# Transposing on the DMA crossbar in place of TensorE, in a fused linear-attention and MLP layer

## The chip, the cores and the metric

The kernel runs on one core of a Trainium2 chip. A core has five engines that run side by side, each with its own queue of instructions: TensorE (PE in the profile: matmuls and transposes; PEld is its loading of weights), VectorE (DVE), ScalarE (ACT), GpSimd (POOL) and SyncE (SP), which here only issues DMAs. The DMAs of a core share 16 DMA engines. Data lives in SBUF, 128 partitions wide; TensorE writes its results to PSUM, from where VectorE or ScalarE takes them. The metric is the device time of one execution, in microseconds (us), as a median of several runs.

## The reference

Input are 2048 tokens of 512 features, all in bf16. The tokens are normalised, and both branches read the normalised tokens:

```python
xn = layernorm(x)                                    # [2048, 512]
# branch A: linear attention, 32 heads of 16
q, k, v = split(xn @ wqkv)
phi(t)  = concat(softmax(t @ w_phi), softmax(-t @ w_phi))   # per head, 16 -> 32
kv, z   = phi(k).T @ v, sum over tokens of phi(k)    # per head, over all 2048 tokens
o       = (phi(q) @ kv) / (phi(q) @ z + 1e-6)        # [2048, 512]
# branch B: MLP with 1792 hidden units
h       = mish(xn @ w1 + b1)
out     = x + o @ wo + h @ w2
```

Since kv and z are sums over all tokens, no attention output can be made before the last token has been seen.

## The kernel before

The tokens are worked on in four groups of 512, each of four tiles of 128 tokens (TPG = 4). All weights stay in SBUF. There are two phases.

The first phase takes the groups in turn. `stage_ln(g)` makes the statistics of four tiles (L178, L179), the reciprocal deviations (L182, L186) and the normalised tile `xn`, tokens on partitions (L188). The matmuls need the features on partitions, so each `xn` of 128 x 512 is transposed by TensorE in four blocks of 128 x 128 (L197) into a PSUM bank `ptr`, and ScalarE copies two tiles at a time (L202) into `xnT`, one buffer per group, two buffers in turn. `xnT` is the weight operand of keys and values (`stage_kv_pair`, L252 and L267, two tiles of tokens at a time) and the moving operand, 512 tokens wide, of queries (`stage_q`, L328) and of the hidden layer (`stage_h`, L364, 56 matmuls a group). ScalarE makes the exponentials (L260, L261, L336, L337) and mish (L374); VectorE makes sums, reciprocals and products. `stage_kvacc` (L303) adds the group's share of kv and z. `stage_ln` of the next group is called between `stage_q` and `stage_kvacc` of the present one, so the next `xnT` is made while the hidden layer of the present group runs.

The second phase takes the groups again. `stage_o(g)` makes, per tile of 128 tokens, numerators and denominators (L389, eight matmuls, into one of the two double PSUM banks), a reciprocal (L398) and the product `o_t` (L400). The four `o_t` of a group are transposed by TensorE (L412, 16 transposes into two banks `ptro`) and copied by ScalarE (L417) into `oT`. `stage_out(g)` loads the group's tokens again for the residual (L422), and adds for each tile 14 matmuls with w2 (L427) and four with wo, whose weight operand is `oT` (L435), in one PSUM bank; VectorE adds the residual (L443), SyncE stores (L444).

The order in which each engine runs its instructions is fixed when the kernel is built, by the framework's scheduler, which starts from the order of the program and moves ready work forward into gaps; the waits between engines are put in by it too. ScalarE's functions are held in the order written (`chain`). The DMAs of the later token loads (L471), of the residuals (L422) and of the stores (L444) go through SyncE's queue, in order. The buffers of tokens (`xg`) are two, so a load waits until the tile that lay there has been read.

Of the kernel before, what the change touches and what calls it, by code (L numbers as in the profile page):

```python
# [8 lines left out]
BF16 = mybir.dt.bfloat16  # L9
# [8 lines left out]
def kernel(  # L18
# [12 lines left out]
    nc = tc.nc  # L31
    P = 128
    S, D, NH, DH, F = 2048, 512, 32, 16, 1792
    NG = 4
    TPG = 4
    NT = NG * TPG
    KT = D // P
# [22 lines left out]
    xnTpool = ctx.enter_context(tc.tile_pool(name="xnT", bufs=2))  # L60
# [15 lines left out]
    with nc.allow_non_contiguous_dma(reason="tiny w_phi load"):  # L76
# [19 lines left out]
    ident = consts.tile([P, P], BF16, name="ident")  # L96
# [8 lines left out]
        out=mask17[:],  # L105
        in_=mask17[:],
# [7 lines left out]
        out=mask17[:],  # L114
        in_=mask17[:],
# [46 lines left out]
    def bank_m(name, shape=None, dt=FP32):  # L162
        return ps_m.tile(shape or [P, 512], dt, name=name, tag="m")


    def stage_ln(g):
        xg = xgs[g]
        mv = spool.tile([P, TPG, nc.vector.BN_AGGR_DIM], FP32, name="mv")
        rstd = spool.tile([P, TPG], FP32, name="rstd")
        xnT = xnTpool.tile([P, KT, 512], BF16, name="xnT")  # L170
        step = 1 if g == 0 else TPG
        for t0 in range(0, TPG, 2):
            ptr = bank_m("ptr", [P, KT, 2 * P], BF16)
            for t in range(t0, t0 + 2):
                if t % step == 0:
                    for u in range(t, t + step):
                        st = spool.tile([P, nc.vector.BN_STATS_DIM], FP32, name="st")
                        nc.vector.bn_stats(st[:], xg[:, u, :])  # L178
                        nc.vector.bn_aggr(mv[:, u, :], st[:])  # L179
                    us = slice(t, t + step)  # L180
                    chain(
                        nc.scalar.activation(  # L182
                            rstd[:, us], mv[:, us, 1], ACT.Sqrt, bias=eps_t[:]
                        )
                    )
                    nc.vector.reciprocal(rstd[:, us], rstd[:, us])  # L186
                xn = xnpool.tile([P, D], BF16, name="xn")
                nc.vector.tensor_scalar(  # L188
                    out=xn[:],
                    in0=xg[:, t, :],  # L190
                    scalar1=mv[:, t, 0:1],
                    scalar2=rstd[:, t : t + 1],
                    op0=ALU.subtract,
                    op1=ALU.mult,
                )
                for kt in range(KT):
                    nc.tensor.transpose(  # L197
                        ptr[:, kt, (t - t0) * P : (t - t0 + 1) * P],
                        xn[:, kt * P : (kt + 1) * P],
                        ident[:],  # L200
                    )
            nc.scalar.copy(xnT[:, :, t0 * P : (t0 + 2) * P], ptr[:])  # L202
        return xnT


# [41 lines left out]
    def stage_kv_pair(xnT, pr):  # L247
        pk = big("pk")
        for tt in range(2):
            tok0 = (2 * pr + tt) * P  # L250
            for kt in range(KT):
                nc.tensor.matmul(  # L252
                    pk[:, tt, :],
                    lhsT=xnT[:, kt, tok0 : tok0 + P],
                    rhs=wkp[:, kt, :],
                    start=(kt == 0),
                    stop=(kt == KT - 1),
                )
        ek = ekpool.tile([P, 2, 2, 512], BF16, name="ek")
        chain(nc.scalar.activation(ek[:, 0], pk[:], ACT.Exp))  # L260
        chain(nc.scalar.activation(ek[:, 1], pk[:], ACT.Exp, scale=-1.0))  # L261
        v12s = []
        for tt in range(2):
            tok0 = (2 * pr + tt) * P
            pv = bank_v("pv")
            for kt in range(KT):
                nc.tensor.matmul(  # L267
                    pv[:],
                    lhsT=xnT[:, kt, tok0 : tok0 + P],
                    rhs=wv[:, kt, :],  # L270
                    start=(kt == 0),
                    stop=(kt == KT - 1),
                )
            ss = spool.tile([P, 2, NH], FP32, name="ss")
            nc.vector.reduce_sum(  # L275
                ss[:],
                ek[:, :, tt, :].rearrange("p s (h e) -> p s h e", e=DH),
                axis=AX.X,
            )
            rk = spool.tile([P, 2, NH], FP32, name="rk")  # L280
            nc.vector.reciprocal(rk[:], ss[:])
            v12 = vpool.tile([P, 2, NH, VW], BF16, name="v12")
            nc.vector.tensor_tensor(
                out=v12[:, :, :, 0:DH],
                in0=pv[:]
                .rearrange("p (o h e) -> p o h e", o=1, e=DH)
                .to_broadcast([P, 2, NH, DH]),
                in1=rk[:, :, :, None].to_broadcast([P, 2, NH, DH]),
                op=ALU.mult,
            )  # L290
            nc.gpsimd.tensor_copy(v12[:, :, :, DH], rk[:])
            v12s.append(v12)
        return ek, v12s
# [27 lines left out]
    def stage_q(g, xnT):  # L321
        gs = slice(g * 512, (g + 1) * 512)
        for jp in range(2):
            pq = big("pq")
            for jj in range(2):
                j = 2 * jp + jj
                for kt in range(KT):
                    nc.tensor.matmul(  # L328
                        pq[:, jj, :],
                        lhsT=wqp[:, kt, j * P : (j + 1) * P],  # L330
                        rhs=xnT[:, kt, :],
                        start=(kt == 0),
                        stop=(kt == KT - 1),
                    )
            eq = eqpool.tile([P, 2, 2, 512], BF16, name="eq")
            chain(nc.scalar.activation(eq[:, 0], pq[:], ACT.Exp))  # L336
            chain(nc.scalar.activation(eq[:, 1], pq[:], ACT.Exp, scale=-1.0))  # L337
            for jj in range(2):
                j = 2 * jp + jj
                for pl in range(2):  # L340
                    pS = bank_m("pS")
                    nc.tensor.matmul(  # L342
                        pS[:],
                        lhsT=B16b[:],
                        rhs=eq[:, 1 - pl, jj, :],
                        start=True,
                        stop=True,
                    )
                    nc.vector.tensor_tensor(  # L349
                        out=eqT[:, pl * 4 + j, gs],  # L350
                        in0=pS[:],
                        in1=eq[:, pl, jj, :],
                        op=ALU.mult,
                    )


    def stage_h(xnT, pool):
        act = pool.tile([P, FT, 512], BF16, name="act")
        for fp in range(FT // 2):
            ph = big("ph")  # L360
            for ff in range(2):
                f = 2 * fp + ff
                for kt in range(KT):
                    nc.tensor.matmul(  # L364
                        ph[:, ff, :],
                        lhsT=w1_sb[:, kt, f * P : (f + 1) * P],
                        rhs=xnT[:, kt, :],
                        start=(kt == 0),
                        stop=(kt == KT - 1),
                    )  # L370
            for ff in range(2):
                f = 2 * fp + ff
                chain(
                    nc.scalar.activation(  # L374
                        act[:, f, :], ph[:, ff, :], ACT.Mish, bias=b1f[:, f : f + 1]
                    )
                )
        return act


    def stage_o(g):
        oT = oTpool.tile([P, 4, 512], BF16, name="oT")
        o_ts = []
        for t in range(TPG):
            tok0 = g * 512 + t * P
            pnd = big("pnd")
# [16 lines left out]
                in1=rd[:, :, :, None].to_broadcast([P, 2, 16, DH]),  # L403
                op=ALU.mult,
            )
            o_ts.append(o_t)
        for jh in range(2):
            ptr = bank_m("ptro", [P, 2, 512], BF16)
            for t in range(TPG):
                for jj in range(2):  # L410
                    j = 2 * jh + jj
                    nc.tensor.transpose(  # L412
                        ptr[:, jj, t * P : (t + 1) * P],
                        o_ts[t][:, j * P : (j + 1) * P],
                        ident[:],
                    )
            nc.scalar.copy(oT[:, 2 * jh : 2 * jh + 2, :], ptr[:])  # L417
        return oT

    def stage_out(g, act, oT):  # L420
        xg2 = xpool.tile([P, TPG, D], BF16, name="xg")
        nc.sync.dma_start(xg2[:], x_g[g])  # L422
        for t in range(TPG):
# [10 lines left out]
            for j in range(4):  # L434
                nc.tensor.matmul(  # L435
                    po[:],
                    lhsT=oT[:, j, ts],
                    rhs=wo_sb[:, j, :],
                    start=False,
                    stop=(j == 3),  # L440
                )
# [81 lines left out]
```

## Time and profile before

| | us |
|---|---|
| median of 3 timed runs | 212.46 (212.35 to 212.74) |
| the profiled execution | 212.4 |
| its span, from the first to the last instruction | 210.7 |
| TensorE busy | 193.6 (92%) |
| VectorE busy | 117.8 (56%) |
| ScalarE busy | 104.5 (50%) |
| granted TensorE clock, mean | 0.997 of full speed |

A share of busy time is an average over the whole span. The chain that ended last tells which work set the end: it is followed back from the last instruction, at each step to what released it. A wait is idle time of an engine together with what ended it. The ends of matmuls are modelled and overlap, so the distance from one start to the next is the time that a matmul takes of TensorE.

### The profile page before, as it was taken

The page shows a single profiled execution, that of the slowest core. Times are in us where ns is not written, and L with a number is a line of the kernel's source. Part 1 is how long each engine was busy: PE and PEld are TensorE (multiplying, and loading weights), DVE is VectorE, ACT ScalarE, POOL GpSimd, SP SyncE. Part 2 cuts the span into 40 slices and gives each one's busy share as a digit, 9 for nine tenths or more (in the row PEclk, how much of TensorE's full clock was granted, in tenths as well). Part 3 has the DMA queues.
Part 4 walks back from the last instruction along what each step waited for, and adds up shares of the span by engine and source line. Part 5 has one row for each costly group of instructions (what it writes and reads, how often), then busy time and mean ns, then how long its engine had stood idle before and what let it go on. Part 6 is the DMA issues. An engine that isn't in the chain of part 4 may idle for free.

```text
span 210.7 us, 2908 instructions
## 1 busy us (share of the span) xinstructions
PE 193.6 (92%) x1185; PEld 98.0 (47%) x1185; DVE 117.8 (56%) x205; ACT 104.5 (50%) x133; POOL 8.6 (4%) x25
## 2 busy tenths in 40 slices
PE   0398899999989999989999999999999999999993
PEld 0364443564434644435643445644554464455441
DVE  1807799983998505997219985531352172136211
ACT  2565998558895768976589734430030003002100
POOL 2000010000110000110001100000000000000000
PEclk9999999999999999999999999999999999999998
DMA  5999500030000300000200000001030130100010
GB/s 170 342 370 348 170 0 0 2 103 0 2 0 0 102 0 0 0 3 1 98 0 3 0 2 0 3 0 50 28 124 25 50 124 4 50 25 28 25 50 25
DMA packets 12088, 12.25 MB, mean 58 GB/s; under 512 B 1068, under 2 KB 12076, under 8 KB 12076
## 3 DMA queue, kind: packets, MB, share of 16 engines
q1 hardware_dynamic: 10492, 11.02, 15.9%
q10 hardware_dynamic: 1584, 1.07, 1.8%
q8 instruction: 9, 0.15, 0.3%
q14 instruction: 3, 0.02, 0.0%
HBM read 9.98 MB, written 2.10 MB: 57 GB/s over the span
## 4 chain that ended last, share of the span: by engine, by line
PE 71%; ACT 10%; DVE 9%; DMA 7%; issue 1%; SPq 0%; ACTq 0%
PE po L427 23%; PE ph L364 18%; PE po L435 7%; DVE ss L275 5%; DMA xg<-in_A_x_dram 5%; PE pkv L303 4%; PE pnd L389 4%; PE pk L252 3%; PE pv L267 3%; PE pS L342 3%; DMA wk_raw<-in_A_wqkv_dram 2%; ACT ek L261 2%; PE ptro L412 2%; ACT eq L337 2%; PE pq L328 2%; PE ptr L197 1%
## 5 line engine op out<-in xcount | busy, mean ns | idle before, releaser
L364 PE MATMUL ph<-xnT,w_sb 128*128 128x512 bf16 x224 | 55.5, 379 | 1.4 <-ACT act L374 1.4
L427 PE MATMUL po<-w_sb,act 128*128 128x512 bf16 x224 | 54.4, 379 | 0.0
L374 ACT ACTIVATE act<-ph,b1f 128x512 bf16<-128x512 f32 x56 | 35.2, 686 | 22.9 <-PE ph L364 22.9
L443 DVE TENSOR_TENSOR y<-po,xg 128x512 bf16<-128x512 f32 x16 | 11.1, 692 | 46.8 <-PE po L435 46.8
L364 PEld LDWEIGHTS <-w_sb 128*128 128x128 bf16 x224 | 21.6, 98 | 27.2 <-issue 3.4
L417 ACT COPY oT<-ptro 128x1024 bf16<-128x1024 bf16 x8 | 7.7, 1015 | 53.5 <-PE ptro L412 53.5
L427 PEld LDWEIGHTS <-act 128*128 128x128 bf16 x224 | 21.3, 98 | 22.2
L275 DVE TENSOR_REDUCE ss<-ek 128x64 f32<-128x1024 bf16 x16 | 18.7, 1203 | 18.5 <-ACT ek L261 18.5
L349 DVE TENSOR_TENSOR eqT<-pS,eq 128x512 bf16<-128x512 f32 x32 | 20.6, 685 | 1.8 <-PE pS L342 1.6
L267 PE MATMUL pv<-wv,xnT 128*128 128x512 bf16 x64 | 17.3, 396 | 0.0
L435 PE MATMUL po<-wo_sb,oT 128*128 128x512 bf16 x64 | 17.2, 380 | 0.0
L328 PE MATMUL pq<-xnT,wqp 128*128 128x512 bf16 x64 | 15.1, 379 | 1.6 <-ACT ek L261 1.5
L178 DVE BATCH_NORM_STATS2 st<-xg 128x6 f32<-128x512 bf16 x16 | 10.4, 673 | 9.9 <-DMA xg<-in_A_x_dram 9.9
L252 PE MATMUL pk<-wkp,xnT 128*128 128x512 bf16 x64 | 15.8, 379 | 0.0
L197 PE MATMUL ptr<-ident,xn 128*128 128x128 bf16 x64 | 5.9, 243 | 8.7 <-DVE xn L188 8.7
L342 PE MATMUL pS<-eq,B16b 128*128 128x512 bf16 x32 | 11.6, 378 | 0.4 <-DVE eqT L349 0.4
L400 DVE TENSOR_TENSOR o_t<-pnd,rd 128x512 bf16<-128x512 f32 x16 | 11.1, 691 | 0.6
L328 PEld LDWEIGHTS <-wqp 128*128 128x128 bf16 x64 | 6.2, 97 | 9.7 <-issue 2.8
L267 PEld LDWEIGHTS <-xnT 128*128 128x128 bf16 x64 | 6.4, 102 | 7.2 <-issue 0.7
L435 PEld LDWEIGHTS <-oT 128*128 128x128 bf16 x64 | 5.6, 98 | 8.9 <-ACT oT L417 3.2
L389 PEld LDWEIGHTS <-eqT 128*128 128x128 bf16 x128 | 7.9, 98 | 3.8 <-DVE o_t L400 2.4
L389 PE MATMUL pnd<-kvm,eqT 128*128 128x136 bf16 x128 | 9.6, 223 | 0.0
(102 smaller groups left out, 199.2 us busy)
## 6 DMA issues: line engine op xcount, KB each, us to landing
xg<-in_A_x_dram SPq DMA_DIRECT2D x7, 512.0 KB, 3.8
out_dram<-y SPq DMA_DIRECT2D x16, 128.0 KB, 1.7
w_sb<-in_B_w_dram SPq DMA_DIRECT2D x2, 896.0 KB, 9.1
w_sb<-in_B_w_dram SPq DMA_DIRECT2D x1, 1792.0 KB, 14.7
wk_raw<-in_A_wqkv_dram ACTq DMA_DIRECT2D x1, 512.0 KB, 4.8
xg<-in_A_x_dram SPq DMA_DIRECT2D x2, 256.0 KB, 4.4
wv<-in_A_wqkv_dram SPq DMA_DIRECT2D x1, 512.0 KB, 7.6
wq_raw<-in_A_wqkv_dram ACTq DMA_DIRECT2D x1, 512.0 KB, 8.5
```

The lines of the kernel that those rows point to most:

```text
L252: nc.tensor.matmul(pk[:, tt, :], lhsT=xnT[:, kt, tok0 : tok0 + P], rhs=wkp[:, kt, :], start=(kt == 0), stop=(kt == KT - 1),)
L267: nc.tensor.matmul(pv[:], lhsT=xnT[:, kt, tok0 : tok0 + P], rhs=wv[:, kt, :], start=(kt == 0), stop=(kt == KT - 1),)
L275: nc.vector.reduce_sum(ss[:], ek[:, :, tt, :].rearrange("p s (h e) -> p s h e", e=DH), axis=AX.X,)
L328: nc.tensor.matmul(pq[:, jj, :], lhsT=wqp[:, kt, j * P : (j + 1) * P], rhs=xnT[:, kt, :], start=(kt == 0), stop=(kt == KT - 1),)
L342: nc.tensor.matmul(pS[:], lhsT=B16b[:], rhs=eq[:, 1 - pl, jj, :], start=True, stop=True,)
L349: nc.vector.tensor_tensor(out=eqT[:, pl * 4 + j, gs], in0=pS[:], in1=eq[:, pl, jj, :], op=ALU.mult,)
L364: nc.tensor.matmul(ph[:, ff, :], lhsT=w1_sb[:, kt, f * P : (f + 1) * P], rhs=xnT[:, kt, :], start=(kt == 0), stop=(kt == KT - 1),)
L374: nc.scalar.activation(act[:, f, :], ph[:, ff, :], ACT.Mish, bias=b1f[:, f : f + 1])
L389: nc.tensor.matmul(pnd[:, j // 2, (j % 2) * 136 : (j % 2) * 136 + 136], lhsT=eqT[:, pl * 4 + j, tok0 : tok0 + P], rhs=kvm[:, pl * 4 + j, : ...
L400: nc.vector.tensor_tensor(out=o_t[:].rearrange("p (a h e) -> p a h e", a=2, e=DH), in0=nd[:, :, :, 0:DH], in1=rd[:, :, :, None].to_broadca ...
L427: nc.tensor.matmul(po[:], lhsT=act[:, f, ts], rhs=w2_sb[:, f, :], start=(f == 0), stop=False,)
L435: nc.tensor.matmul(po[:], lhsT=oT[:, j, ts], rhs=wo_sb[:, j, :], start=False, stop=(j == 3),)
```

## The change

For groups 1 to 3 the four normalised tiles of a group, and for all groups the four `o_t`, are no longer transposed by TensorE and copied by ScalarE. Each tile of 128 x 512 goes through one DMA on SyncE's queue (`dma_start_transpose`) from SBUF to SBUF, transposed on the way. The first group's normalised tiles stay on TensorE. Since one DMA writes a whole tile, `xnT` and `oT` are laid out tile by tile: [128, tile, block of features, 128 tokens] in place of [128, block of features, 512 tokens]. The moving operand of L328 and L364 therefore becomes four runs of 128 columns.

```diff
--- before.py
+++ after.py
@@ -167,10 +167,10 @@
         xg = xgs[g]
         mv = spool.tile([P, TPG, nc.vector.BN_AGGR_DIM], FP32, name="mv")
         rstd = spool.tile([P, TPG], FP32, name="rstd")
-        xnT = xnTpool.tile([P, KT, 512], BF16, name="xnT")
+        xnT = xnTpool.tile([P, TPG, KT, P], BF16, name="xnT")
         step = 1 if g == 0 else TPG
         for t0 in range(0, TPG, 2):
-            ptr = bank_m("ptr", [P, KT, 2 * P], BF16)
+            ptr = bank_m("ptr", [P, 2, KT, P], BF16) if g == 0 else None
             for t in range(t0, t0 + 2):
                 if t % step == 0:
                     for u in range(t, t + step):
@@ -193,13 +193,15 @@
                     op0=ALU.subtract,
                     op1=ALU.mult,
                 )
+                if g > 0:
+                    nc.sync.dma_start_transpose(out=xnT[:, t], in_=xn[:])
+                    continue
                 for kt in range(KT):
                     nc.tensor.transpose(
-                        ptr[:, kt, (t - t0) * P : (t - t0 + 1) * P],
-                        xn[:, kt * P : (kt + 1) * P],
-                        ident[:],
-                    )
-            nc.scalar.copy(xnT[:, :, t0 * P : (t0 + 2) * P], ptr[:])
+                        ptr[:, t - t0, kt, :], xn[:, kt * P : (kt + 1) * P], ident[:]
+                    )
+            if g == 0:
+                nc.scalar.copy(xnT[:, t0 : t0 + 2], ptr[:])
         return xnT
 
 
@@ -247,11 +249,10 @@
     def stage_kv_pair(xnT, pr):
         pk = big("pk")
         for tt in range(2):
-            tok0 = (2 * pr + tt) * P
             for kt in range(KT):
                 nc.tensor.matmul(
                     pk[:, tt, :],
-                    lhsT=xnT[:, kt, tok0 : tok0 + P],
+                    lhsT=xnT[:, 2 * pr + tt, kt, :],
                     rhs=wkp[:, kt, :],
                     start=(kt == 0),
                     stop=(kt == KT - 1),
@@ -261,12 +262,11 @@
         chain(nc.scalar.activation(ek[:, 1], pk[:], ACT.Exp, scale=-1.0))
         v12s = []
         for tt in range(2):
-            tok0 = (2 * pr + tt) * P
             pv = bank_v("pv")
             for kt in range(KT):
                 nc.tensor.matmul(
                     pv[:],
-                    lhsT=xnT[:, kt, tok0 : tok0 + P],
+                    lhsT=xnT[:, 2 * pr + tt, kt, :],
                     rhs=wv[:, kt, :],
                     start=(kt == 0),
                     stop=(kt == KT - 1),
@@ -328,7 +328,7 @@
                     nc.tensor.matmul(
                         pq[:, jj, :],
                         lhsT=wqp[:, kt, j * P : (j + 1) * P],
-                        rhs=xnT[:, kt, :],
+                        rhs=xnT[:, :, kt, :],
                         start=(kt == 0),
                         stop=(kt == KT - 1),
                     )
@@ -364,7 +364,7 @@
                     nc.tensor.matmul(
                         ph[:, ff, :],
                         lhsT=w1_sb[:, kt, f * P : (f + 1) * P],
-                        rhs=xnT[:, kt, :],
+                        rhs=xnT[:, :, kt, :],
                         start=(kt == 0),
                         stop=(kt == KT - 1),
                     )
@@ -379,8 +379,7 @@
 
 
     def stage_o(g):
-        oT = oTpool.tile([P, 4, 512], BF16, name="oT")
-        o_ts = []
+        oT = oTpool.tile([P, TPG, 4, P], BF16, name="oT")
         for t in range(TPG):
             tok0 = g * 512 + t * P
             pnd = big("pnd")
@@ -403,18 +402,7 @@
                 in1=rd[:, :, :, None].to_broadcast([P, 2, 16, DH]),
                 op=ALU.mult,
             )
-            o_ts.append(o_t)
-        for jh in range(2):
-            ptr = bank_m("ptro", [P, 2, 512], BF16)
-            for t in range(TPG):
-                for jj in range(2):
-                    j = 2 * jh + jj
-                    nc.tensor.transpose(
-                        ptr[:, jj, t * P : (t + 1) * P],
-                        o_ts[t][:, j * P : (j + 1) * P],
-                        ident[:],
-                    )
-            nc.scalar.copy(oT[:, 2 * jh : 2 * jh + 2, :], ptr[:])
+            nc.sync.dma_start_transpose(out=oT[:, t], in_=o_t[:])
         return oT
 
     def stage_out(g, act, oT):
@@ -434,7 +422,7 @@
             for j in range(4):
                 nc.tensor.matmul(
                     po[:],
-                    lhsT=oT[:, j, ts],
+                    lhsT=oT[:, t, j, :],
                     rhs=wo_sb[:, j, :],
                     start=False,
                     stop=(j == 3),
```

## Rows read from the trace of the kernel before

**Rows 1.** The page's busy us, share of the span, instructions, by engine

```profile
PE 193.6 (92%) x1185; PEld 98.0 (47%) x1185; DVE 117.8 (56%) x205; ACT 104.5 (50%) x133; POOL 8.6 (4%) x25
```

**Rows 2.** The page's chain that ended last, shares of the span by engine

```profile
PE 71%; ACT 10%; DVE 9%; DMA 7%; issue 1%; SPq 0%; ACTq 0%
```

**Rows 3.** Stretches; columns as their header line says

```profile
core 0: us, PE busy (x) PEld busy (x) DVE busy (x) ACT busy (x) POOL busy (x), PEclk, DMA share, GB/s
47.30:76.40 29.10, 27.84 (x162) 13.63 (x161) 20.08 (x33) 22.38 (x28) 1.79 (x4) 1.00 0.06 19
151.10:169.80 18.70, 18.70 (x124) 9.51 (x122) 6.59 (x12) 1.93 (x2) 0.00 (x0) 1.00 0.17 57
```

**Rows 4.** The chain in order of time, first phase: start us, us, what

```profile
41.03 1.01 PE ptr L197 x16
...
69.44 0.85 PE ptr L197 x12
70.50 0.22 PE ptr L197 x4
70.72 0.43 PE ph L364 x2
71.15 0.79 PE pkv L303 x12
```

**Rows 5.** The timeline, first phase: start us, us, engine, line, work, [idle before]

```profile
74.87 1.27 ACT L374 ACTIVATE act<-ph,b1f 128x512 bf16<-128x512 f32 x2 [1.77 <-PE ph L364]
```

**Rows 6.** The same chain in the output phase, groups 1 to 3

```profile
151.09 0.95 PE pnd L389 x16
152.04 0.86 PE po L427 x4
152.90 0.61 PE pnd L389 x8
153.51 0.22 PE ptro L412 x4
...
157.33 0.52 PE po L435 x2
...
162.00 3.02 PE po L427 x14
165.02 0.86 PE po L435 x4
...
169.77 0.95 PE pnd L389 x16
...
188.51 0.95 PE pnd L389 x16
```

**Rows 7.** ScalarE's copies by line: busy, mean ns, idle before

```profile
L417 ACT COPY oT<-ptro 128x1024 bf16<-128x1024 bf16 x8 | 7.7, 1015 | 53.5 <-PE ptro L412 53.5
L202 ACT COPY xnT<-ptr 128x1024 bf16<-128x1024 bf16 x8 | 7.7, 1014 | 1.1 <-PE ptr L197 1.1
```

**Rows 8.** DMA issues to landing (us): the page's, then L422's own

```profile
xg<-in_A_x_dram SPq DMA_DIRECT2D x7, 512.0 KB, 3.8
out_dram<-y SPq DMA_DIRECT2D x16, 128.0 KB, 1.7
...
DMA to landing us min/median/max: 3.3/3.4/4.3
```

**Rows 9.** The timeline of group 1's normalised tiles and their first readers

```profile
40.22 1.37 DVE L188 TENSOR_SCALAR xn<-xg,mv,rstd 128x512 bf16<-128x512 bf16 x4
...
47.32 1.89 PE L252 MATMUL pk<-wkp,xnT 128*128 128x512 bf16 x8
...
50.78 1.89 PE L252 MATMUL pk<-wkp,xnT 128*128 128x512 bf16 x8
```

**Rows 10.** The timeline of VectorE and SyncE at the first o_t of group 1

```profile
152.12 0.69 DVE L400 TENSOR_TENSOR o_t<-pnd,rd 128x512 bf16<-128x512 f32 x1
152.23 0.43 SPq L422 DMA_DIRECT2D xg<-in_A_x_dram  x1
```

## The prediction, made before the changed kernel was run

> **What bounds the kernel now.** I read the page's busy shares first. TensorE is busy 92% of the span, ScalarE 50% [rows 1]. Because that is an average over stages, I read the chain that ended last next: 71% of it is TensorE and 10% ScalarE [rows 2]. TensorE time that goes therefore counts, unless the stage it leaves is held by something else. The table of stretches tells which stage is which. A period of the first phase (one group of 512 tokens) lasts 29.10 us with TensorE busy for 27.84, so 1.3 us per group are waits; a group of the output phase lasts 18.70 us and TensorE is busy in all of it [rows 3]. The output phase is bound by TensorE alone, the first phase nearly so.
>
> **What goes from TensorE in the first phase.** Groups 1 to 3 lose 16 transposes each. In the chain in order of time, the 16 of group 1 take 1.01 us in one piece. Those of group 2 start at 69.44 and the next stage (L303) at 71.15: 1.71 us, of which three L364 matmuls are 0.65 (two take 0.43), so 1.06 us belong to the transposes and their waits for VectorE [rows 4]. Group 3 repeats this pattern. Sum: 1.01 + 1.06 + 1.06 = 3.1 us. Does it shorten the stage? What follows is L364, whose results ScalarE evacuates; ScalarE there sits idle for 1.77 us waiting for TensorE [rows 5], so earlier matmuls do make the stretch earlier. With the transposes go two copies of 1.01 us per group on ScalarE; I price them at nothing, because that same idle time follows them. If all of that cover were gone they would be worth up to 2.0 us a group more.
>
> **What goes in the output phase.** From the first L389 of group 1 (151.09) to that of group 2 (169.77) is 18.68 us, to that of group 3 (188.51) 18.74 [rows 6]. The matmuls that stay are 72 of L427 and L435, 18 per token tile, at 3.02 us for 14 and 0.86 for 4, so 4 x 3.88 = 15.52 us; and 32 of L389 at 0.95 us for 16, so 1.90 us [rows 6]. Together 17.42, so 1.26 us per group belong to the 16 transposes (0.22 us for four, 0.88 in all) and 0.38 to waits. Of the waits, those for the two o_t tiles that free the PSUM buffers stay (the piece of eight L389 takes 0.61 instead of 0.475, and a second one like it): I leave 0.2 in place. Gain: 1.05 a group, 4.2 us for four, if I price group 0 like the others. The eight L417 copies of 1.015 us lie on a ScalarE that has nothing else to do here [rows 7]; they cost no throughput, only latency.
>
> **What comes in their place.** 28 DMAs on SyncE's queue, 12 in the first phase and 16 in the output phase, each of 128 KB out of and into SBUF. No row shows one. The nearest, by bytes, is the output store: 128 KB, 1.7 us to landing. The far end is the 512 KB load of tokens, 3.8 us [rows 8]: a transpose as dear as one plain DMA per block of 128 columns. Below 1.7 us it gains nothing more, since it is hidden at 1.7 already. I take 1.7 us, and one after the other, the nearest row with nothing overlapped.
>
> Is that hidden? First phase, group 1: the four normalised tiles are made from 40.22 on in 1.37 us, the first by 40.56; tiles 0 and 1 are first read at 47.32, tiles 2 and 3 at 50.78 [rows 9]. With 1.0 us of TensorE work gone these become 46.3 and 49.8 (tile 1 at 47.2, tile 3 at 50.6). Landings in series at 42.3, 44.0, 45.7 and 47.4: all early, the tightest by 3.2 us. The work that hides them is the rest of L364 and the 32 matmuls of L303. Output phase, group 1: the first o_t is done at 152.12 + 0.69 = 152.81 [rows 10] and would land at 154.5. TensorE needs it after 32 L389, 14 L427 and the 0.2 of waits, at 151.09 + 1.90 + 3.02 + 0.2 = 156.2. The others come 3.88 us apart on TensorE and 1.7 us apart on the queue. Hidden too, and what is late next is VectorE's o_t, as before.
>
> The queue itself. SyncE issues in order, and a transpose waits there for VectorE, so whatever stands behind it waits as well: the next token load, the residual loads (L422), the output stores. None of these is read soon, except that the order also works the other way. At 152.23 the residual load of a later group goes out, just before the first o_t is ready [rows 10], and it can take 4.3 us to land [rows 8]. A transpose issued behind it on the same queue would then land with it, at about 156.6, 0.4 us after it is needed. The residual buffers come free in this way for groups 2 and 3, so I charge 0.4 twice: 0.8 us.
>
> The moving operand of L328 and L364 becomes four runs of 128 columns. On ScalarE the copy that writes four runs (L202) takes 1014 ns and the one that writes two long ones 1015 [rows 7]: no price. On TensorE the upper bound is four separate instructions of 128 columns, 0.22 us for the four [rows 6] against 0.216 for one of 512 (0.86 for four): 4 ns on 288 matmuls, 1.2 us. Zero is my value.
>
> On the price of one transpose two rules of the Trainium skill disagree. "Advanced Engine Details and Errata", X-Bar Transpose, says that on trn2 a transposing DMA is as fast as a plain one, which fits the store's row. "VectorE: DVE Perf Modes", The three transpose paths, gives 1309 ns for one 128x128 block through the crossbar against 390 ns on TensorE; four in series would be an estimate of 5.2 us per DMA, past the far end above and against this change. By the first page the sum below stays as it is; by the second the slower rival below holds at 5.2 us, and its sum would be an estimate of some 257 us. No row of this trace decides between them.
>
> **Sum.** The profiled execution took 212.4 us (span 210.7 and 1.7 around it), the median of the timed runs is 212.46, so no correction: 212.4 - 3.1 - 4.2 + 0.8 = 205.9 us.
>
> **Rivals.** A slower one: transposes that run one at a time at 3.8 us. The place is the first phase. In group 1 they land at 44.4, 48.2, 52.0 and 55.8; tile 3 is wanted at 50.6, so the stage ends 5.2 us late, of which the 1.3 us of waits that the stretch has anyway hide some: 3.9 us, three times, 11.7 us. In the output phase the first lands at 156.6 instead of 156.2, and the others keep up with the 3.88 us per tile: 0.4 x 4 = 1.6. Time: 212.4 - 7.3 + 11.7 + 1.6 = 218.4. It decides from 3 x (4r - 10.0 - 1.3) = 7.3, that is r = 3.4 us per transpose. For it: the pieces that a transpose moves are small, and 28 of them share one queue. Against: the same bytes as a plain store are half of that.
>
> ScalarE's order sets the first phase. Then L197's time is not given back: 212.4 - 4.2 + 0.8 = 209.0. For it: TensorE already loses 1.3 us per period in the stretch of exponentials. Against: the row that shows ScalarE waiting for TensorE [rows 5].
>
> The transposes of the output phase are late. If the first has to wait for the residual load to land and only then takes its own 1.7 us, it comes at 152.23 + 4.3 + 1.7 = 158.2, 2.0 late, in two groups: 212.4 - 7.3 + 4.0 = 209.1. For it: one queue, in order. Against: the load's landing time holds a fixed part that need not stand in the way of what follows it (a quarter of its bytes lands in 1.7 us).
>
> No change in sum: part of the slower rival with r near 3.4.
>
> **How the numbers follow.** The forecast has 50%; its own range is 204.0 (a third of the ScalarE copies counts, 0.6 us a group) to 207.5 (the 1.2 us of strided reads, and 0.4 more of late tiles). The ScalarE rival has 12%, the late output transposes 13%, no change 5%, the slower one 20%. What a measurement here can tell from no change is 0.2%, 0.4 us. Faster: 50 + 12 + 13 = 75%; same 5%; slower 20%. The range of 8 in 10 goes from 203.6, with a few per cent below, through both partial rivals and the near end of the slower one to 213.0; r of 3.5 us lies inside it, the rest of that rival outside.
>
> **What would show it.** The changed profile should have 16 matmuls left on L197 and none on L412, no ScalarE copy after the first group, a period of about 17.4 to 17.8 us from L389 to L389, and L252 of groups 1 to 3 starting without a wait for a DMA. A landing time of the transposes near 2 us confirms the price; waits of L252, L328 or L364 on xnT show the slower rival, waits of L435 on oT the late one. ScalarE idle no longer than before ahead of L374, with the first phase as long as before, shows the ScalarE rival. A transpose of 3.4 us or more on the queue, or 288 matmuls that stream slower, would make the prediction wrong.

## The result, and the profile after

The changed kernel takes 206.76 us (median of 4 runs, 206.52 to 206.78) where the kernel before takes 212.6 beside it: ratio 0.972, 95% interval 0.971 to 0.974. The forecast was 205.9 with a range of 203.6 to 213.0. The profiled execution took 206.8 us, its span is 205.1 at a granted clock of 0.999, so it stands for the median.

The page of the changed kernel: busy time by engine, DMA queue (packets, MB, share of 16 engines), the chain that ended last; and, from the view of DMAs, the issues of the transposes with the median us to landing.

```profile
PE 185.3 (90%) x1073; PEld 92.5 (45%) x1073; DVE 117.3 (57%) x205; ACT 91.4 (45%) x119; POOL 8.6 (4%) x25
...
q1 hardware_dynamic: 25724, 14.69, 28.0%
...
PE 52%; DVE 22%; DMA 13%; ACT 6%; issue 5%; SPq 1%; ACTq 0%
...
L374 ACT ACTIVATE act<-ph,b1f 128x512 bf16<-128x512 f32 x56 | 35.2, 684 | 27.5 <-PE ph L364 27.5
...
oT<-o_t SPq DMA_TRANSPOSE x16, 2.4
xnT<-xn SPq DMA_TRANSPOSE x12, 2.5
```

TensorE runs 112 instructions fewer and is busy for 8.3 us less [rows 1]; ScalarE runs 14 fewer, 13.1 us less, and in front of L374 it now waits for TensorE for 27.5 us. Before, that row read:

```profile
L374 ACT ACTIVATE act<-ph,b1f 128x512 bf16<-128x512 f32 x56 | 35.2, 686 | 22.9 <-PE ph L364 22.9
```

But the chain holds 22% VectorE and 13% DMA where it held 9% and 7% [rows 2]: something new is late. A transpose lands 2.4 us after it is issued, between the two bounds of [rows 8]; the plain loads and stores land as before.

The table of stretches shows where: first phase of groups 1 and 2, then the four output groups.

```profile
core 0: us, PE busy (x) PEld busy (x) DVE busy (x) ACT busy (x) POOL busy (x), PEclk, DMA share, GB/s
46.10:75.30 29.20, 26.79 (x145) 12.82 (x144) 21.32 (x36) 20.65 (x26) 1.78 (x4) 1.00 0.23 39
75.30:102.90 27.60, 26.64 (x145) 12.82 (x144) 18.74 (x28) 20.54 (x26) 1.74 (x4) 1.00 0.17 39
130.80:147.60 16.80, 16.78 (x102) 8.38 (x101) 6.08 (x11) 1.26 (x2) 0.00 (x0) 1.00 0.28 56
147.60:165.80 18.20, 17.69 (x105) 8.73 (x104) 6.59 (x12) 0.00 (x0) 0.00 (x0) 1.00 0.34 87
165.80:183.90 18.10, 17.73 (x105) 8.78 (x104) 6.59 (x12) 0.00 (x0) 0.00 (x0) 1.00 0.33 87
183.90:201.70 17.80, 17.75 (x105) 8.76 (x103) 6.60 (x13) 0.00 (x0) 0.00 (x0) 1.00 0.24 60
```

Group 1's period of the first phase, 29.2 us, is as long as before [rows 3] although TensorE does 1.05 us less in it; group 2's is 1.1 shorter. Output groups 1 and 2 have 0.4 to 0.5 us in which TensorE is idle; groups 0 and 3 next to none.

The timeline says what group 1 waits for: rows of VectorE, TensorE and SyncE (start us, us, engine, line, work, idle before).

```profile
40.25 1.37 DVE L188 TENSOR_SCALAR xn<-xg,mv,rstd 128x512 bf16<-128x512 bf16 x4
...
50.24 1.29 DVE L178 BATCH_NORM_STATS2 st<-xg 128x6 f32<-128x512 bf16 x2 [5.16 <-DMA xg<-in_A_x_dram]
...
52.98 1.19 DVE L275 TENSOR_REDUCE ss<-ek 128x64 f32<-128x1024 bf16 x1
...
46.09 1.89 PE L253 MATMUL pk<-wkp,xnT 128*128 128x512 bf16 x8
...
49.54 1.89 PE L253 MATMUL pk<-wkp,xnT 128*128 128x512 bf16 x8
...
40.68 5.96 SPq L197 DMA_TRANSPOSE xnT<-xn  x4
46.69 0.58 SPq L459 DMA_DIRECT2D xg<-in_A_x_dram  x1
```

The transposes themselves are in time: both L253 pieces start without a wait, 1.2 us earlier than in [rows 9]. But four transposes hold SyncE's queue for 5.96 us, and the token load of group 3 (L459) stands behind them. It goes out at 46.69 and lands at 50.2. VectorE, in order, waits 5.16 us for it, and the sums over exponentials (L275), which stand behind the statistics, are late; TensorE then waits for VectorE at L267; in the table of waits (us in all, times, longest) this is TensorE's longest of the stretch:

```profile
PE pv L267 <- DVE v_594 L283: 1.4, 1, 1.4
```

In the output phase, the chain in order of time (start us, us, what):

```profile
149.46 3.77 DMA oT<-o_t
153.23 0.05 issue
153.28 1.04 PE po L423 x4
...
165.97 0.95 PE pnd L388 x16
166.92 0.85 PE po L415 x4
167.77 3.57 DMA oT<-o_t
```

And SyncE's timeline at group 1:

```profile
148.85 0.43 SPq L410 DMA_DIRECT2D xg<-in_A_x_dram  x1
149.46 5.14 SPq L405 DMA_TRANSPOSE oT<-o_t  x4
```

Where the residual load (L410) is issued just before it, the first transpose of a group takes 3.6 to 3.8 us to land instead of 2.4, and L423 waits 0.4 to 0.5 us.

### The profile page after: what moved, and what is told of

The parts are those of the page before. It is cut to its first block, busy times and chain, and to the rows that moved or that the text cites. A ratio compares the mean times of both kernels' runs of the same rounds, so it can differ in the third digit from the quotient of the medians.

```text
span 205.1 us, 2739 instructions
## 1 busy us (share of the span) xinstructions
PE 185.3 (90%) x1073; PEld 92.5 (45%) x1073; DVE 117.3 (57%) x205; ACT 91.4 (45%) x119; POOL 8.6 (4%) x25
## 4 chain that ended last, share of the span: by engine, by line
PE 52%; DVE 22%; DMA 13%; ACT 6%; issue 5%; SPq 1%; ACTq 0%
PE po L415 21%; PE ph L364 11%; PE po L423 7%; DMA xg<-in_A_x_dram 7%; DVE eqT L349 5%; DVE ss L275 5%; DMA oT<-o_t 4%; DVE st L178 3%; PE pk L253 3%; PE pv L267 3%; PE pnd L388 2%; DMA wk_raw<-in_A_wqkv_dram 2%; DVE xn L188 2%; ACT ek L262 2%; PE pkv L303 2%
## 5 line engine op out<-in xcount | busy, mean ns | idle before, releaser
L364 PE MATMUL ph<-xnT,w_sb 128*128 128x512 bf16 x224 | 55.0, 379 | 0.5 <-ACT act L374 0.5
L415 PE MATMUL po<-w_sb,act 128*128 128x512 bf16 x224 | 52.4, 379 | 0.0
L374 ACT ACTIVATE act<-ph,b1f 128x512 bf16<-128x512 f32 x56 | 35.2, 684 | 27.5 <-PE ph L364 27.5
L364 PEld LDWEIGHTS <-w_sb 128*128 128x128 bf16 x224 | 21.6, 98 | 27.2 <-issue 3.1
L275 DVE TENSOR_REDUCE ss<-ek 128x64 f32<-128x1024 bf16 x16 | 18.7, 1200 | 16.7 <-ACT ek L262 16.7
L267 PE MATMUL pv<-wv,xnT 128*128 128x512 bf16 x64 | 16.6, 385 | 1.4 <-DVE v_594 L283 1.4
L423 PE MATMUL po<-wo_sb,oT 128*128 128x512 bf16 x64 | 16.5, 379 | 0.9 <-DMA oT<-o_t 0.9
L328 PE MATMUL pq<-xnT,wqp 128*128 128x512 bf16 x64 | 15.1, 379 | 1.6 <-ACT ek L262 1.5
L253 PE MATMUL pk<-wkp,xnT 128*128 128x512 bf16 x64 | 15.8, 379 | 0.0
L328 PEld LDWEIGHTS <-wqp 128*128 128x128 bf16 x64 | 6.2, 97 | 9.7 <-issue 2.8
L267 PEld LDWEIGHTS <-xnT 128*128 128x128 bf16 x64 | 6.3, 100 | 8.5 <-issue 1.9
L423 PEld LDWEIGHTS <-oT 128*128 128x128 bf16 x64 | 6.0, 98 | 9.1 <-DMA oT<-o_t 2.2
L388 PEld LDWEIGHTS <-eqT 128*128 128x128 bf16 x128 | 8.2, 98 | 3.8 <-DVE o_t L399 2.3
L200 PE MATMUL ptr<-ident,xn 128*128 128x128 bf16 x16 | 2.0, 311 | 8.7 <-DVE xn L188 8.7
L388 PE MATMUL pnd<-kvm,eqT 128*128 128x136 bf16 x128 | 9.6, 223 | 0.0
L261 ACT ACTIVATE ek<-pk 128x1024 bf16<-128x1024 f32 x8 | 8.2, 1029 | 2.3 <-ACT ek L262 2.1
```

The lines of the kernel that those rows point to most:

```text
L253: nc.tensor.matmul(pk[:, tt, :], lhsT=xnT[:, 2 * pr + tt, kt, :], rhs=wkp[:, kt, :], start=(kt == 0), stop=(kt == KT - 1),)
L267: nc.tensor.matmul(pv[:], lhsT=xnT[:, 2 * pr + tt, kt, :], rhs=wv[:, kt, :], start=(kt == 0), stop=(kt == KT - 1),)
L275: nc.vector.reduce_sum(ss[:], ek[:, :, tt, :].rearrange("p s (h e) -> p s h e", e=DH), axis=AX.X,)
L328: nc.tensor.matmul(pq[:, jj, :], lhsT=wqp[:, kt, j * P : (j + 1) * P], rhs=xnT[:, :, kt, :], start=(kt == 0), stop=(kt == KT - 1),)
L364: nc.tensor.matmul(ph[:, ff, :], lhsT=w1_sb[:, kt, f * P : (f + 1) * P], rhs=xnT[:, :, kt, :], start=(kt == 0), stop=(kt == KT - 1),)
L374: nc.scalar.activation(act[:, f, :], ph[:, ff, :], ACT.Mish, bias=b1f[:, f : f + 1])
```

## The experiments

The theory after these rows: (a) a transpose costs SyncE 1.2 us and lands in 2.4, which is hidden; (b) the shortfall of the first phase is the token load behind the four transposes; (c) that of the output phase is the residual load ahead of the first transpose. Rivals: the strided moving operand, the bytes in flight rather than the order of the queue, and late transposes.

I compare distances between stages: from the first L253 of a group to that of the next, and for group 3 to the first L388 (the periods of groups 1 to 3 of the first phase); then from the first L388 of a group to that of the next, and for the last group to VectorE's last addition (output groups 0 to 3). Before: 29.07, 28.74, 27.81, then 17.99, 18.68, 18.73, 18.94. After: 29.22, 27.61, 27.83, then 16.80, 18.26, 18.11, 17.77.

**One half at a time.** e1_ln_only keeps the normalised tokens' transposes and puts the outputs back on TensorE; e2_o_only the reverse.

```diff
--- after.py
+++ e1_ln_only.py
-            nc.sync.dma_start_transpose(out=oT[:, t], in_=o_t[:])
+            o_ts.append(o_t)
...
+                    nc.tensor.transpose(
+                        ptr[:, jj, t * P : (t + 1) * P],
...
+            nc.scalar.copy(oT[:, 2 * jh : 2 * jh + 2, :], ptr[:])
--- after.py
+++ e2_o_only.py
-                if g > 0:
-                    nc.sync.dma_start_transpose(out=xnT[:, t], in_=xn[:])
-                    continue
...
-            if g == 0:
-                nc.scalar.copy(xnT[:, t0 : t0 + 2], ptr[:])
+            nc.scalar.copy(xnT[:, t0 : t0 + 2], ptr[:])
```

> Only the normalised tiles of groups 1 to 3 go through the crossbar; the attention outputs are transposed by TensorE as before. Theory (the two halves are independent; the first phase gives 3.3 us back and loses 1.1 to the token load that stands behind four transposes on SyncE's queue): first L253 of group 3 some 2.2 us earlier than before, output phase unchanged, 210.3 us. Rival (the two halves share a loss, so that one alone does better than its part): under 209.8 us.

> Only the attention outputs go through the crossbar; all normalised tiles are transposed by TensorE, into the new layout with four runs of 128 columns. Theory: first phase as before to 0.2 us (so the four runs cost TensorE nothing), output phase 3.4 us shorter, groups 1 and 2 with less gain (0.4 to 0.6) than groups 0 and 3 (1.2): 209.1 us. Rival (the strided moving operand costs time): first phase longer than before by up to 1.2 us, 210.3 us.

e1 took 211.12 us (ratio 0.995, 0.993 to 0.996), e2 210.53 (0.991, 0.989 to 0.993). Both fell short, and 1.3 + 1.9 is not 5.8: the halves don't add. e1's periods are 29.65, 27.62, 27.82: shortfall (b) alone, in group 1. e2's first phase, with the strided operand in all its matmuls of queries and of the hidden layer, has 29.07, 28.73, 27.82, equal to before's: the strided operand costs nothing. e2's group 0 gained nothing (18.06 us against 16.80 in the changed kernel); that is half of the 2.6 us that are missing. The rest is a first phase that starts 0.4 us later in e2 than before, one that is 0.6 us longer in e1 than in the changed kernel, and 0.4 us at e1's end, behind VectorE's last addition; no run shows the cause of the first and the last. Its timeline on SyncE and TensorE shows why, and the line's durations (ns min/median/max):

```profile
135.08 6.49 SPq L401 DMA_TRANSPOSE oT<-o_t  x4
...
138.83 1.04 PE L419 MATMUL po<-wo_sb,oT 128*128 128x512 bf16 x4 [1.12 <-DMA oT<-o_t]
```

```profile
L401 SPq DMA_TRANSPOSE oT<-o_t x16: 1200/1216/2574, 135.1 to 193.8; - x16
```

The first transpose of the program holds the queue for 2.57 us, not 1.2.

**The long hold.** First guess: a start-up cost. e5_o_only_warm is e2 with one small transpose into a spare tile near 15 us.

```diff
+    warmT = consts.tile([P, 1, 16], BF16, name="warmT")
+    nc.sync.dma_start_transpose(out=warmT[:], in_=ident[0:16, :])
```

> Attention outputs alone through the crossbar, as in the second experiment, with one small transpose of 16 rows of the identity, read by nobody, issued on SyncE near 16 us. Theory (the first transpose of a program holds SyncE 2.0 to 2.6 us in place of 1.2, whichever it is; in the second experiment that one was the first output tile, and TensorE waited 1.1 us for it): the small transpose takes the long hold, the first output tile is held 1.2 us, group 0 of the output phase falls from 18.06 to some 16.9 us, 209.4 us. Rival (group 0 was late for another reason, such as ScalarE's or VectorE's work at the border of the phases): group 0 stays at 18.06, 210.5 us.

209.68 us (0.987, 0.985 to 0.989). The number came near; the reason fell. The first tile after the small one still held the queue 2.29 us, and group 0 lasted 17.76, not 16.8. Most of the gain over e2 is a start of group 1 that is 1.05 us earlier (46.63 against 47.68); the first L253 of group 0 is as much earlier already, and no run shows why.

Going through all transposes by their start gave another theory. In the changed kernel the long ones are not the first: they are the third of groups 1 and 2 and the first of group 3 (43.34, 71.98 and 96.91 us; 1.98, 1.72 and 1.70 us long), and at 43.9, 72.4 and 97.3 queue q8 loads a 16 KB block of instructions. In e2 one is loaded at 135.9, inside the long hold; in e5 at 134.9, likewise. e12_fetch_moved is e2 with 32 idle transposes on TensorE at the start, so that these loads fall elsewhere.

```diff
--- e2_o_only.py
+++ e12_fetch_moved.py
+    pad = bank_m("pad", [P, P], BF16)
+    for _ in range(32):
+        nc.tensor.transpose(pad[:], ident[:], ident[:])
     xnTs[0] = stage_ln(0)
```

> The output half alone (as e2), with 32 more 128x128 transposes of the identity on TensorE while it waits for the first tokens; their result is not read. What makes one transpose in a stretch hold SyncE for 2.0 to 2.6 us? Theory A: a block of instructions that is loaded at the same moment (queue q8). In e2 one is loaded at 135.8 us, inside the long hold of 135.08 to 137.65; the 64 more TensorE instructions should bring the loads some 5 us forward: to about 131, 153 and 173. Then the first output tile holds the queue 1.2 us, group 0 lasts 16.9 instead of 18.06, a tile of groups 1 and 2 has the long hold instead, where it is mostly hidden, and the time is about 209.3. Theory B: the first large transpose of a program is the long one, whatever is loaded: 2.3 to 2.6 us at the first output tile again, group 0 of 17.8 to 18.1, about 210.5.

The total missed: 214.28 us (1.010, 1.007 to 1.012). Group 0 began at 136.50 us instead of 133.30: with the extra work TensorE has a wait of 4.27 us for VectorE at 19.6 us, and the granted clock was 0.89 from 15 to 30; how much either cost, no run isolates. The hold behaved as theory A says. Blocks are loaded at 132.1, 153.5, 176.3 and 197.0 us; no transpose of groups 0 and 1 is over 1.3 us long, and group 0 lasts 16.89 us. The long ones are now at 176.21 (1.80 us) and 197.11 (1.95). SyncE's timeline of the four groups, and the line's waiters:

```profile
138.28 5.33 SPq L401 DMA_TRANSPOSE oT<-o_t  x4
...
155.36 5.12 SPq L401 DMA_TRANSPOSE oT<-o_t  x4
...
173.62 5.71 SPq L401 DMA_TRANSPOSE oT<-o_t  x4
...
193.21 5.86 SPq L401 DMA_TRANSPOSE oT<-o_t  x4
```

```profile
L401 SPq DMA_TRANSPOSE oT<-o_t x16: 1194/1216/1949, 138.3 to 197.1; - x16
...
  PE po L419: 2.4, 2
```

One expectation failed here too: the long hold was not hidden in group 2. There a residual load, the transposes and the block meet, TensorE waits 1.8 us for oT, and the group lasts 19.59 us (18.12 in e2).

So a transpose that is under way while a block of instructions is loaded can be stretched from 1.2 to between 1.7 and 2.6 us. The other traces agree: in all runs together 30 transposes hold the queue for more than 1.5 us, and every one of them overlaps the loading of a block. Not every block does it: one loaded in e3 at 98.17 us and one in e6 at 97.95 lengthened a hold by at most 0.2. In the full change the long hold falls on one tile of each first-phase group and costs only what stands behind it. In group 1 that is the token load: in e1 and e6 this tile holds the queue for 2.39 and 2.26 us in place of 1.98, and the period is 29.65 and 29.56 us in place of 29.22.

**The token load.** e3_tokens_on_pool issues all token loads of L459 on GpSimd, e7_token3_on_pool only group 3's; e9_token3_early issues group 3's near 17 us, on SyncE, into a buffer of oT that is free until the output phase.

```diff
--- after.py
+++ e3_tokens_on_pool.py
-                nc.sync.dma_start(xgs[g + 1][:], x_g[g + 1])
+                nc.gpsimd.dma_start(xgs[g + 1][:], x_g[g + 1])
--- after.py
+++ e7_token3_on_pool.py
-                nc.sync.dma_start(xgs[g + 1][:], x_g[g + 1])
+                (nc.gpsimd if g + 1 == 3 else nc.sync).dma_start(xgs[g + 1][:], x_g[g + 1])
--- after.py
+++ e9_token3_early.py
+            xg3 = oTpool.tile([P, TPG, 4, P], BF16, name="oT")
+            xgs[3] = xg3[:].rearrange("p t j q -> p t (j q)")
+            nc.sync.dma_start(xgs[3], x_g[3])
...
-            if g + 1 > 1:
+            if g + 1 == 2:
```

> The changed kernel with the token loads of groups 2 and 3 issued on GpSimd's queue in place of SyncE's. Theory (the load of group 3 was late because it stood behind four transposes in the queue, 1.2 us each, and VectorE, in order, waited with it): the load goes out near 41.6 and not 46.7, VectorE no longer waits for it at 50, the period from L253 of group 1 to that of group 2 falls from 29.2 to 28.0 us; 205.6 us. Rival (the crossbar holds the 16 DMA engines, so the load lands late whatever queue issues it): VectorE waits as before, 206.8 us.

> The changed kernel with the token load of group 3 alone on GpSimd's queue; that of group 2 stays on SyncE, so the start is as in the changed kernel. Theory (in the third experiment the start was 2 us later because the load of group 2 went out at 10 us beside the weights, and only group 1's period, 27.8 in place of 29.2 us, belongs to the queue): first L253 of group 1 at 46.1, period 27.8, 205.4 us. Rival (the later start itself gave the shorter period): period near 29, 206.6 us.

> The changed kernel with the tokens of group 3 loaded near 20 us into one of the two oT buffers, which nothing else uses until the output phase, on SyncE's queue as before. Moved to GpSimd's queue the load had gone out at 42.0, among the transposes, and the second tile of group 1 came late in its place, so it was not the queue's order alone but also the bytes in flight. Theory (load and transposes are in each other's way wherever they meet; apart, both are free): no wait of VectorE for that load, no wait of L253 for xnT, period from group 1 to group 2 28.0 us in place of 29.2, 205.5 us. Rival (the 1.2 us come from the order of VectorE's statistics or from TensorE's order, not from the load): period 29.2, 206.8 us.

e3: 207.62 us (0.980, 0.975 to 0.984). Its group 1 has a period of 27.77, as (b) says, but the phase began 2.05 us late: on GpSimd's queue the load of group 2 went out at 10.2 us, among the weights, where SyncE's order had held it until 15.5; I take that for the cause, no run isolates it. e7, in which the start is as in the changed kernel: 207.58 (0.977, 0.975 to 0.979), a miss: period 29.35. Its TensorE, then the landing of the transposes of xnT:

```profile
46.15 1.03 PE L253 MATMUL pk<-wkp,xnT 128*128 128x512 bf16 x4
48.75 1.04 PE L253 MATMUL pk<-wkp,xnT 128*128 128x512 bf16 x4 [1.57 <-DMA xnT<-xn]
```

```profile
DMA to landing us min/median/max: 2.5/3.5/5.6
```

With the load (issued at 41.99) beside the transposes instead of behind them, the second tile, issued at 42.13, was there for TensorE only at 48.75; the third landed 5.6 us after its issue, with a block of instructions loaded beside it too. In e3 the second tile was as slow (5.4 us to landing), and only the later start hid it, so e3's short period does not show that another queue helps. The order of the queue is thus half the story; the load and the transposes hinder each other on whatever queue they start. e9, which moves the load away from both, took 205.23 us (0.966, 0.964 to 0.967) with a period of 27.62. SyncE's timeline:

```profile
17.09 1.39 SPq L462 DMA_DIRECT2D xg<-in_A_x_dram  x1
40.72 5.71 SPq L197 DMA_TRANSPOSE xnT<-xn  x4
46.48 0.57 SPq L410 DMA_DIRECT2D xg<-in_A_x_dram  x1
```

The four transposes take nearly as long (5.71 us), but only a residual load that nobody needs soon stands behind them. That confirms (b): in the changed kernel the load's place behind the transposes is what costs the time. e7 adds that a place beside them costs as much.

**The residual load.** e4_all_loads_on_pool is e3 with the residual loads on GpSimd too; e6_residual_early keeps them on SyncE but gives those of groups 2 and 3 a buffer (a dead eq) that comes free in the first phase.

```diff
--- e3_tokens_on_pool.py
+++ e4_all_loads_on_pool.py
-        nc.sync.dma_start(xg2[:], x_g[g])
+        nc.gpsimd.dma_start(xg2[:], x_g[g])
--- after.py
+++ e6_residual_early.py
+        if g < 2:
+            xg2 = xpool.tile([P, TPG, D], BF16, name="xg")
+        else:
+            xg2 = eqpool.tile([P, 2, 2, 512], BF16, name="eq")
+            xg2 = xg2[:].rearrange("p a b d -> p (a b) d")
```

> The changed kernel with the token loads and the residual loads on GpSimd's queue, so that only transposes and stores are left on SyncE's. Theory (a residual load just ahead of the first transpose of groups 1 and 2 makes it land 3.6 to 3.9 us after issue in place of 2.4): first transpose of each group lands in 2.4 us, no wait of L423, groups 1 and 2 as long as group 3 (17.6 us), 204.4 us. Rival (the load's bytes hold the same DMA engines): first transposes of groups 1 and 2 still land after 3.5 us or more, 205.6 us.

> The changed kernel with the residual loads of groups 2 and 3 in the two buffers of the query exponentials, dead by then, so that they go out before the output phase and none stands next to a transpose. Theory (the load's 512 KB, just ahead of the first transpose of groups 1 and 2, make it land 3.6 to 3.9 us after issue): it lands in 2.4 us, groups 1 and 2 fall from 18.26 and 18.2 to 17.6 us each, 205.5 us. Rival (the first transpose of these groups is late because VectorE finishes the group before at the same time): no change, 206.8 us.

e4: 208.52 us (0.982, 0.978 to 0.986). Its first phase begins 3.6 us later than the changed kernel's, so the total says little; its output groups 1 and 2 last 18.24 and 18.29, no shorter than there. The load now leaves on another queue, at the same point of the group (GpSimd, SyncE, TensorE):

```profile
150.92 0.75 POOL L410 DMA_DIRECT2D xg<-in_A_x_dram  x1 [31.90 <-DVE rd L397]
...
151.64 5.13 SPq L405 DMA_TRANSPOSE oT<-o_t  x4
...
155.45 1.04 PE L423 MATMUL po<-wo_sb,oT 128*128 128x512 bf16 x4 [0.50 <-DMA oT<-o_t]
```

The wait is the same 0.50 us: it is the load in flight, not its queue. e6: 205.77 us (0.968, 0.967 to 0.970), groups 1 and 2 at 17.57 each, and no wait of TensorE in the output phase. So (c) holds, with the rival's reason.

**The price of a transpose.** e8_split issues each tile as two transposes of 64 KB: the same bytes, twice the instructions.

```diff
--- after.py
+++ e8_split.py
...
-            nc.sync.dma_start_transpose(out=oT[:, t], in_=o_t[:])
+            for h in range(2):
+                nc.sync.dma_start_transpose(
+                    out=oT[:, t, 2 * h : 2 * h + 2], in_=o_t[:, h * 256 : h * 256 + 256]
+                )
```

> The changed kernel with each transpose cut into two of 256 columns: 56 DMAs of 64 KB in place of 28 of 128 KB. Theory (a transpose holds SyncE 1.2 us whatever its size, so a tile costs 2.4 us): in group 1 the last half lands near 52.3, 1.9 us after it is first read, and the token load goes out at 51 and lands at 54.7, 4.4 us later than in the changed kernel, all of it on VectorE's way; groups 2 and 3 lose some 0.6 each, the first output tile of each group 1.1 or less: some 216 us. Rival (the hold goes by bytes): 206.8 us.

215.94 us (1.016, 1.014 to 1.017): slower than the kernel before. Its timeline on SyncE and VectorE, then both lines' holds (ns min/median/max):

```profile
40.66 11.47 SPq L198 DMA_TRANSPOSE xnT<-xn  x8
52.19 0.57 SPq L465 DMA_DIRECT2D xg<-in_A_x_dram  x1
...
55.73 1.29 DVE L178 BATCH_NORM_STATS2 st<-xg 128x6 f32<-128x512 bf16 x2 [10.67 <-DMA xg<-in_A_x_dram]
```

```profile
L198 SPq DMA_TRANSPOSE xnT<-xn x24: 1170/1240/2382, 40.7 to 114.7; - x24
...
L409 SPq DMA_TRANSPOSE oT<-o_t x32: 1167/1224/1982, 142.0 to 204.1; - x32
```

Half the bytes hold SyncE as long as the whole (1.24 and 1.22 us): the hold belongs to the instruction. The total was forecast, its terms were not. Against the changed kernel group 1's period is 6.4 us longer (35.62; 4.4 were expected), the other two 1.5 each, output group 0 0.7, while groups 1 and 2 (17.77 and 17.73) are 0.4 to 0.5 shorter: there the first half tile, behind the residual load, lands 3.3 and 3.2 us after its issue, where the whole tile took 3.8 and 3.6, and TensorE doesn't wait for oT.

**Both loads early.** e10_both_early joins e6 and e9; e11_before_early makes the same two moves in the kernel before.

> The changed kernel with both moved: the tokens of group 3 into an oT buffer near 20 us, and the residual loads of groups 2 and 3 into the two buffers of the query exponentials before the output phase. Theory (two independent costs of the change, each a load that met a transpose): 1.2 and 1.0 us come back, 204.5 us. Rival (they hide one another): 205.5 us.

> The kernel before with the same two moves of loads and no crossbar. Theory (without transposes on the queue no load was late): as before within 0.3 us, 212.4 us. Rival (the moves are worth as much without the transposes): 210.3 us.

e10: **203.99 us** (0.960, 0.959 to 0.961), faster than both kernels and 0.5 better than expected; e11: 212.56 (1.000, 0.9995 to 1.001). The moves are worth nothing by themselves; they only take away what the transposes brought. e10's stretches, groups 1 and 2 of the first phase and 0 to 2 of the output:

```profile
46.28:73.89 27.61, 26.55 (x143) 12.84 (x144) 20.37 (x35) 20.53 (x26) 1.78 (x4) 1.00 0.22 42
73.89:101.50 27.61, 26.55 (x143) 12.82 (x144) 18.74 (x28) 20.54 (x26) 1.74 (x4) 1.00 0.17 41
...
129.32:146.09 16.77, 16.65 (x99) 8.39 (x100) 6.09 (x11) 1.27 (x2) 0.00 (x0) 1.00 0.31 56
146.09:163.66 17.57, 17.46 (x103) 8.86 (x104) 6.59 (x12) 0.00 (x0) 0.00 (x0) 1.00 0.24 61
163.66:181.24 17.58, 17.48 (x104) 8.85 (x105) 6.59 (x12) 0.00 (x0) 0.00 (x0) 1.00 0.24 60
```

Both periods are now alike, and in the output phase TensorE is idle for 0.1 us a group.

## Why the prediction was right

**First phase: gain 3.1 forecast, 2.2 measured** (group 0's first L388 at 132.94 before and 130.75 after). Its three terms: before group 1's L253, 1.0 forecast, 1.23 measured; group 1's period, which lost group 2's transposes, 1.06 forecast, -0.15 measured; group 2's period 1.06 forecast, 1.13 measured. The step that failed is the queue: "None of these is read soon" was not true of the token load. The prediction priced what the transposes do to TensorE and did not follow the load behind them to VectorE. e9 gives the size of the error: with the load out of the way the same terms are 1.19, 1.45 and 1.13, 3.8 us in sum. So the gross gain was set too low by 0.7, the cost of the queue at nothing instead of 1.6.

**Output phase: 4.2 - 0.8 = 3.4 forecast, 3.4 measured** (1.19, 0.42, 0.62 and 1.17 us by group). The net number is exact partly by cancellation: by e6, where groups 1 and 2 don't wait, the gross gain is 132.94 to 207.28 against 131.07 to 200.76, so 74.34 - 69.69 = 4.65; the residual load takes back 1.25, not 0.8. The mechanism was right, for the two loads that were named: the transpose issued at 149.46 landed at 153.23, half a us behind the load issued ahead of it.

Over both phases the gross gain was set too low by 1.1 us and the cost of the loads by 2.0. That the forecast came within 0.9 us of the measured time is in part luck.

**The price of a transpose.** 1.7 us in series was taken; the runs show two numbers for it, 1.2 us of the queue and 2.4 to landing. In series that is a pace of 1.3, so the tiles of the first phase were early, and those of the output phase wherever no load was in flight. Of the Trainium skill's two rules that of "Advanced Engine Details and Errata", X-Bar Transpose, as fast as a plain DMA, is the nearer, though a plain store of these bytes lands in 1.7 us. The 1309 ns per 128x128 block of the Trainium skill's "VectorE: DVE Perf Modes", The three transpose paths, taken four times as in the prediction's 5.2 us, is not what the runs show: a tile of four blocks lands in 2.4 us, and one leaves the queue every 1.3. No run transposes a single block.

**The slower rival** was not the case, but its mechanism is real, and at a lower price than 3.4 us: in e8 a tile costs the queue 2.4 us and the kernel is slower than before. The rival's sum left out the token load, too. **ScalarE's order** does not set the first phase: ScalarE waits for TensorE more than before, and in e9 the periods shrink by all that TensorE no longer does. **Late output transposes** would have given 2.0 us twice; the wait is 0.5 us, since the transpose lands half a us after the load and not 1.7 after it. **The strided operand** is free (e2).

## What to carry to other kernels

When work moves to a DMA queue, price how long each instruction holds the queue, then list what stands behind it, with its reader and what waits behind that reader: here 6 us of transposes made one load late, and an engine that works in order passed the delay on to work that doesn't use the load. Look also at the big loads that are in flight at that moment on any queue: moving three of them (a token load and two residual loads) to a time when no transpose is in flight was worth 2.8 us here, moving them to another queue lost 0.8 to 1.8. One half of a change tried alone need not give half of the gain.

## What the runs showed of the hardware

A transposing DMA from SBUF to SBUF holds SyncE for 1.2 us whether it moves 64 or 128 KB; a plain 128 KB store holds it 0.33. A 128 KB transpose is 544 packets: 28 of them are the 15,232 by which q1 grew, from 10,492 to 25,724. A 512 KB load started just before delays the landing from 2.4 us to between 3.6 and 4.0 in the output groups, on whichever queue it was started (3.8 on GpSimd's, in e4). The loading of a block of instructions stretches the hold by 0.5 to 1.4 us, with the two exceptions above; it delays landings as well, to 4.0 us in e9 for a transpose of group 1 with no such load near it. Where load and block met, up to 5.6 us were measured (e7). Which of the resources they share does that, no run here shows.
